# g stored unscaled, scaled by ScalarE after its load: one change to a planned attention and two-layer MoE kernel

## The chip, the cores and the metric

The kernel runs on one core of a Trainium2 chip. The metric is the device time of one execution, in microseconds; the figure for the kernel before is the median of three runs. A profile of one further execution gives the trace that is read here. The engines are named as in the profile: PE is TensorE's matmul, PEld its weight load, DVE is VectorE, ACT is ScalarE, POOL is GpSimd and SP is the queue that issues DMAs.

## The reference

Only the last part matters for this change. Attention (full attention over sequences shortened by four, plus a local one) gives x of 2304 tokens by 512; a first feed-forward layer with an ELU follows; then:

```python
def _moe2_ref(x, w_in, w_out, s, b) -> np.ndarray:
    h = x @ w_in
    r = np.maximum(h, 0.0)
    g = s * (r * r) + b
    return (g @ w_out).astype(np.float32)
```

Here w_in is 512 by 2048 and w_out 2048 by 512; s and b are one number each. All is float32. The kernel makes each product of float32 matrices from three products of a rounded high part and a remainder (high by high, low by high, high by low).

## The kernel before, in words

**A planner orders everything.** The program first collects operations (`op`, `act`, `on`, `load`), each with an engine or several to choose from, a length in microseconds that is written in by hand, the buffers that it reads and writes, and a due time. `Plan.emit` then moves due times back along the dependences, simulates the engines, and at each step gives an engine the operation with the earliest due time that is ready; if a more urgent one is not ready yet, an operation that is ready runs in the pause. The order so found is the order in each engine's instruction stream. Where the simulation sees TensorE idle, `keep_warm` (L1581) puts in matmuls of a tile of zeros, as many as fill the pause.

**The second feed-forward layer has two halves.** In the w2_in half (540 to 735 us) five groups of tokens pass through `unit`: groups 0, 1, 2 and 4 are pairs of 256-token blocks, group 3 is one block alone. A pair's four units each make seven products (`product`, L1453, twelve matmuls each, a scheme of Strassen's kind), in the order `ROW`. The first is copied out of PSUM by ScalarE (L1479), the others are summed by VectorE (`total`, L1463). The single block's unit (L1425) has plain products and returns before `product` is defined. Each finished h of 128 by 512 then goes through Relu on ScalarE (L1473 or L1435) and `finish`: a square (L1401, ScalarE or GpSimd; for one block in four Relu and square in one pass on VectorE, L1404), then a scale and shift by s and b (L1407), then a store to a buffer `gd` in DRAM (L1440, L1474). There are 72 such h. The next group's inputs are split into high and low parts by ScalarE (L1352) and VectorE (L1353).

The w2_out half (735 us to the end) is made of nine quads (`quad`), two for each pair, one for the single block. A quad loads four pieces of g of 128 by 1024 from `gd` (L1500, tile `gb`), and forms seven halves in the order `COL`: some are a loaded piece, others sums and differences of pieces (VectorE, L1527 to L1535). Each half is rounded to its high part by ScalarE (L1509), VectorE subtracts for the low part (L1510), and 24 matmuls follow (L1518). There are three buffers for these parts (`F`), and their places come free as the inputs `X` of the w2_in half are used up; the `gb` places and those of the sums lie where weights and h lay before. The weights of the w2_out half were prepared earlier and kept in DRAM; `kept_halves` loads them again (L1315) and splits them by ScalarE (L1282) and VectorE (L1283), as the places of the w2_in weights come free; pairs of weights 0 to 3 serve the first quad, 4 to 7 the second.

The due time of a quad is `time2[1, gi, qd]`, written `d` in the code; its loads are due 12 us earlier, its halves 2.84 us apart.

Of the kernel before, what the change touches and what calls it, by code (L numbers as in the profile page):

```python
# [299 lines left out]
def attn_moe_moe2(ctx, tc, q, k, v, w_in, w_out, w2_in, w2_out, s2, b2, mask, mask_d, out):  # L300
# [93 lines left out]
    def op(eng, us, fn, r=(), w=(), u=(), due=0.0, dma=0.0, nb=0.0, ffn=False, lock=False):  # L394
        plan.op(eng, us, fn, r, w, u, due, dma, nb, ffn, lock)
# [834 lines left out]
        have = {"dve": (0.08 + n / 960 + fixed, lambda: f(nc.vector)), "pool": (0.3 + n / 490 + fixed, lambda: f(nc.gpsimd))}  # L1230
        op(*[list(z) for z in zip(*[(e, *have[e]) for e in choice])], lock=True, **kw)

    def act(f, n, **kw):
        op("act", 0.1 + n / 1200, f, **kw)

    def parts():
        return Buf(None, "hi", None), Buf(None, "lo", None)
# [93 lines left out]
    def factors(kind, w, i):  # L1331
        return list(w[0 if i in MADE or i == (4 if kind else 3) else 1].part)
# [59 lines left out]
        return x  # L1392

    gd = {}

    def finish(h, made, stores, due, relu=False):

        q, g = Buf(None, "q", None), Buf(None, "g", None)
        if relu:
            op(["act", "pool"], [0.1 + 512 / 1200, 0.3 + 512 / 490],  # L1400
               [lambda: nc.scalar.activation(out=h(), in_=h(), func=ACTF.Square), lambda: nc.gpsimd.tensor_tensor(out=h(), in0=h(), in1=h(), op=ALU.mult)],  # L1401
               r=[made], w=[q], u=[h], due=due)
        else:
            on(lambda e: e.scalar_tensor_tensor(out=h(), in0=h(), scalar=0.0, in1=h(), op0=ALU.max, op1=ALU.mult), 512, ("dve",),  # L1404
               r=[made], w=[q], u=[h], due=due)
        op(["act", "dve"], [0.1 + 512 / 1200, 0.07 + 512 / 1920],
           [lambda: nc.scalar.activation(out=h(), in_=h(), func=ACTF.Identity, scale=sb2[:, 0:1], bias=sb2[:, 1:2]),  # L1407
            lambda: nc.vector.tensor_scalar(out=h(), in0=h(), scalar1=sb2[:, 0:1], scalar2=sb2[:, 1:2], op0=ALU.mult, op1=ALU.add)],
           r=[q, c_sb2], w=[g], u=[h], due=due, lock=True)
        for dst, fn, n in stores:  # L1410
            load(dst, n, fn, due, r=[g], u=[h], slow=SL)

    def unit(gi, u, x, w):

        d = time2[0, gi, u]
        if len(groups[gi]) == 1:
            for f in range(2):
# [12 lines left out]

                made = Buf(None, "made", None)
                op("pe", 24 * MM, pe, r=[*w[2 * u][1].part, *w[2 * u + 1][1].part, *x[0].part, *x[1].part], w=[e],
                   u=[w[2 * u][1], w[2 * u + 1][1], *x], due=d + f * 2 * PP, ffn=True)
                h = Buf(ar, "st", [128, 512])
                act(lambda h=h, e=e: nc.scalar.activation(out=h(), in_=e(), func=ACTF.Relu), 512, r=[e], w=[made], u=[h], due=d + f * 2 * PP)  # L1435
                stores = []
                for n in range(2):
                    dst = gd.setdefault((gi, 0, 2 * n + f), None) or dram_buf(f"gd{gi}_{2 * n + f}", [128, PAIRS, 128])
                    gd[gi, 0, 2 * n + f] = dst
                    stores.append((dst, lambda dst=dst, h=h, n=n: nc.sync.dma_start(  # L1440
                        out=dst.t[:, 2 * u:2 * u + 2, :], in_=h().rearrange("p (q n t) -> p q n t", q=2, n=2)[:, :, n]), 131072))
                finish(h, made, stores, d + f * 2 * PP + 10, True)
            return
        bank = {i: Buf(*{2: (ps_t, "at"), 5: (ps_h, "h"), 3: (ps_h, "h")}.get(i, (ps_a, "acc")), [128, 512]) for i in ROW}

        def product(i):

            def pe():
                ps = bank[i]()
                for q in range(2):  # L1450
                    for c in range(2):
                        for k, (wi, xi) in enumerate(PASSES):
                            nc.tensor.matmul(ps[:, q * 256:(q + 1) * 256], lhsT=factor(0, w[2 * u + q], i, wi, c),  # L1453
                                             rhs=x[i]()[:, xi].rearrange("p (c t) -> p c t", c=2)[:, c],
                                             start=q == c == k == 0, stop=q == c == 1 and k == 2)

            ws = [w[2 * u], w[2 * u + 1]]
            op("pe", 12 * MM, pe, r=[*factors(0, ws[0], i), *factors(0, ws[1], i), *x[i].part], w=[bank[i]],
               u=[x[i], *ws[0], *ws[1]], due=d + ROW.index(i) * PP, ffn=True)

        def total(i, a):
            h = Buf(ar, "st", [128, 512])
            op("dve", 0.08 + 512 / 940, lambda: nc.vector.tensor_tensor(out=h(), in0=bank[i](), in1=a(), op=ALU.add),  # L1463
               r=[bank[i], a], w=[h], due=d + ROW.index(i) * PP)
            return h

        def out(h, blk):
            dst = gd.get((gi, u // 2, blk)) or dram_buf(f"gd{gi}_{u // 2}_{blk}", [128, 2, 512])
            gd[gi, u // 2, blk] = dst
            made = h  # L1470
            if blk != 3:
                made = Buf(None, "made", None)
                act(lambda: nc.scalar.activation(out=h(), in_=h(), func=ACTF.Relu), 512, r=[h], w=[made], u=[h], due=d + 10)  # L1473
            finish(h, made, [(dst, lambda: nc.sync.dma_start(out=dst.t[:, u % 2], in_=h()), 262144)], d + 10, blk != 3)  # L1474

        for i in ROW:
            product(i)
        p1 = Buf(ar, "st", [128, 512])
        act(lambda: nc.scalar.activation(out=p1(), in_=bank[1](), func=ACTF.Copy), 512, r=[bank[1]], w=[p1], due=d)  # L1479
        out(total(2, p1), 0)  # L1480
        u2 = total(6, p1)
        u3, u4 = total(7, u2), total(5, u2)
        out(total(5, u3), 3)
        out(total(4, u3), 1)
        out(total(3, u4), 2)

    def quad(gi, qd, w, m):

        g = groups[gi]
        d = time2[1, gi, qd]  # L1490
        n_qd = len(g)
        tok = 128 * n_qd
        pairs = range(4 * qd, 4 * qd + 4) if n_qd == 2 else range(PAIRS)
# [3 lines left out]
        for blk in (1, 0, 2, 3):  # L1497
            a[blk], got[blk] = Buf(ar, "gb", [128, 1024]), Buf(None, "got", None)
            src = gd[gi, qd, blk]
            load(got[blk], 524288, lambda b=a[blk], src=src: nc.sync.dma_start(out=b(), in_=src.t.rearrange("p a t -> p (a t)")),  # L1500
                 d - 12, r=[src], u=[a[blk]], slow=SL)
        sq = Buf(ar, "sq", [128, 1024])
        s1, s2, s3, s4 = (Buf(None, f"s{i}", None) for i in range(1, 5))

        def half(i, src, r):
            k = COL.index(i)
            f = Buf(ar, "F", [128, 2, 1024], F32R)
            hi, lo = parts()
            act(lambda: nc.scalar.activation(out=f()[:, 0], in_=src(), func=ACTF.Copy), 1024, r=r, w=[hi], u=[f, src], due=d + 2 * k * PP)  # L1509
            on(lambda e: e.tensor_tensor(out=f()[:, 1], in0=src(), in1=f()[:, 0].bitcast(F32), op=ALU.subtract), 1024, ("dve", "pool"),  # L1510
               r=[*r, hi], w=[lo], u=[f, src], due=d + 2 * k * PP)

            def pe():
                for p, pair in enumerate(pairs):
# [9 lines left out]

        half(2, a[1], [got[1]])
        half(1, a[0], [got[0]])
        on(lambda e: e.tensor_tensor(out=sq(), in0=a[2](), in1=a[3](), op=ALU.add), 1024, r=[got[2], got[3]], w=[s1], u=[sq, a[2], a[3]], due=d + 4 * PP)  # L1527
        done = half(5, sq, [s1])
        on(lambda e: e.tensor_tensor(out=sq(), in0=sq(), in1=a[0](), op=ALU.subtract), 1024, r=[s1, got[0], *done], w=[s2], u=[sq, a[0]], due=d + 6 * PP)
        done = half(6, sq, [s2])  # L1530
        on(lambda e: e.tensor_tensor(out=a[2](), in0=a[0](), in1=a[2](), op=ALU.subtract), 1024, r=[s1, got[0], got[2]], w=[s3], u=[a[0], a[2]], due=d + 8 * PP)
        half(7, a[2], [s3])
        on(lambda e: e.tensor_tensor(out=sq(), in0=a[1](), in1=sq(), op=ALU.subtract), 1024, r=[s2, got[1], *done], w=[s4], u=[sq, a[1]], due=d + 10 * PP)
        half(3, sq, [s4])
        half(4, a[3], [got[3]])  # L1535
        if qd < n_qd - 1:
# [28 lines left out]
    for gi in range(len(groups)):  # L1565
        xs = inputs(gi, time2[0, gi, 0])
        for u in range(PAIRS // 2):
            unit(gi, u, xs, w2)
    w2 = [kept_halves(p, time2[1, 0, p // 4] - 12) for p in range(PAIRS)]
    for gi in order2:  # L1570
        ms = {}
        for qd in range(len(groups[gi])):
# [75 lines left out]
```

## Time and profile before

| | us |
|---|---|
| median of three runs (lowest, highest) | 926.96 (924.21, 929.6) |
| profiled execution, its own time | 927.33 |
| span of the profiled execution, first to last instruction | 925.6 |
| PE busy, 8460 matmuls | 910.1 |
| DVE busy | 700.8 |
| ACT busy | 556.7 |
| POOL busy | 392.0 |

The span is 1.73 us shorter than that execution's own time; what lies around it is not in the trace. Busy time of PE holds the matmuls of zeros too, and a matmul at a lower granted clock counts longer. Times in rows are microseconds from the start of the span.

### The profile page before, as it was taken

How to read it: one execution, taken by the hardware profiler on the slowest of the kernel's cores; microseconds unless marked ns; L12 is line 12 of the kernel's file. 1: busy time of each engine (PE TensorE's matmuls, PEld its weight loads, DVE VectorE, ACT ScalarE, POOL GpSimd, SP SyncE). 2: the span in 40 equal slices, each digit the busy share in tenths (PEclk: the TensorE clock that was granted, in tenths of full speed). 3: DMA queues.
4: the chain of work that ended last, by engine and by line, in shares of the span. 5: the costliest groups of instructions: out<-in, count | busy, mean ns of one | idle time of the engine just before them, and what ended most of it. 6: DMA issues, size and time to landing. Idle time of an engine off the chain costs nothing. (4 is left out here: it accounts for less than half of the span.)

```text
span 925.6 us, 21389 instructions
## 1 busy us (share of the span) xinstructions
PE 910.1 (98%) x8460; PEld 872.6 (94%) x8460; DVE 700.8 (76%) x1089; ACT 556.7 (60%) x1208; POOL 392.0 (42%) x353
## 2 busy tenths in 40 slices
PE   8999999999999999999999999998999989999998
PEld 5879999999999999999999999998999989999998
DVE  5467778888887888988635589989546889787775
ACT  5588776554554545444666669887687963433332
POOL 4567657798896769776536653000000000000000
PEclk9699999999999999999999999999999999999999
DMA  9739776544542425434302357898843783353411
GB/s 196 204 115 234 198 188 168 144 135 109 124 123 64 123 75 135 108 86 128 92 1 91 115 172 261 297 311 307 298 143 117 264 291 126 126 161 120 152 36 35
DMA packets 123524, 142.88 MB, mean 154 GB/s; under 512 B 50976, under 2 KB 93984, under 8 KB 123424
## 3 DMA queue, kind: packets, MB, share of 16 engines
q1 hardware_dynamic: 121632, 141.07, 51.7%
q8 instruction: 66, 1.08, 0.5%
q10 hardware_dynamic: 1792, 0.44, 0.2%
q14 instruction: 34, 0.28, 0.1%
HBM read 101.12 MB, written 40.37 MB: 153 GB/s over the span
## 5 line engine op out<-in xcount | busy, mean ns | idle before, releaser
L1034 PE MATMUL acc<-split,w 128*128 128x256 f32 x1728 | 234.9, 284 | 0.0
L1034 PEld LDWEIGHTS acc<-split,w 128*128 128x128 f32 x1728 | 216.5, 188 | 2.9 <-issue 1.9
L988 PE MATMUL h<-split,w 128*128 128x256 f32 x1488 | 205.2, 286 | 1.2 <-DVE work L1012 1.0
L988 PEld LDWEIGHTS h<-split,w 128*128 128x128 f32 x1488 | 188.7, 190 | 4.0 <-DVE work L1012 1.6
L413 POOL TENSOR_TENSOR split<-work,split 128x256 fp32r<-128x256 f32 (+2 forms) x154 | 137.0, 897 | 88.8 <-ACT split L405 72.8
L1518 PE MATMUL acc<-w,attn 128*128 128x256 f32 x864 | 107.1, 281 | 0.4 <-DVE attn L1510 0.4
L1518 PEld LDWEIGHTS acc<-w,attn 128*128 128x128 f32 x864 | 104.4, 189 | 0.8 <-DVE attn L1510 0.7
L405 ACT ACTIVATE split<-work 128x256 fp32r<-128x256 f32 (+2 forms) x162 | 66.7, 423 | 60.7 <-PE acc L1034 31.6
L1012 DVE SCALAR_TENSOR_TENSOR work<-work,h 128x256 f32<-128x256 f32 x124 | 50.6, 414 | 66.3 <-ACT work L1010 66.0
L1453 PE MATMUL acc<-attn,w 128*128 128x256 f32 x768 | 99.8, 283 | 0.6 <-ACT attn L1352 0.4
L1453 PEld LDWEIGHTS acc<-attn,w 128*128 128x128 f32 x768 | 95.2, 188 | 1.2 <-ACT attn L1352 0.6
L1008 ACT ACTIVATE work<-h 128x256 f32<-128x256 f32 x124 | 47.1, 380 | 75.8 <-PE h L988 48.7
L1509 ACT ACTIVATE attn<-split 128x1024 fp32r<-128x1024 f32 x43 | 45.5, 1060 | 74.5 <-PE acc L1518 29.8
L413 POOL TENSOR_TENSOR work<-work 128x896 f32<-128x896 f32 (+1 forms) x41 | 68.0, 1666 | 6.2 <-DVE work L930 5.5
L1510 DVE TENSOR_TENSOR attn<-split,attn 128x1024 fp32r<-128x1024 f32 x43 | 52.4, 1221 | 19.9 <-ACT attn L1509 19.6
L930 DVE TENSOR_REDUCE work<-work 128x128 f32<-128x896 f32 x36 | 63.5, 1789 | 4.8 <-POOL work L413 4.8
L1010 ACT ACTIVATE work<-work 128x256 f32<-128x256 f32 x144 | 60.0, 416 | 3.9
L1518 PE MATMUL h<-w,attn 128*128 128x256 f32 x432 | 56.1, 286 | 3.1 <-ACT attn L1509 2.4
L1518 PEld LDWEIGHTS h<-w,attn 128*128 128x128 f32 x432 | 54.1, 194 | 3.5 <-ACT attn L1509 2.6
L1407 ACT ACTIVATE split<-split,sb 128x512 f32<-128x512 f32 x64 | 50.7, 809 | 5.6 <-DVE split L1404 4.8
L1453 PE MATMUL h<-attn,w 128*128 128x256 f32 x384 | 51.5, 282 | 0.0
L1283 POOL TENSOR_TENSOR w<-work,w 128x1024 fp32r<-128x1024 f32 x16 | 40.5, 2540 | 20.9 <-ACT w L1282 20.9
(191 smaller groups left out, 1559.6 us busy)
## 6 DMA issues: line engine op xcount, KB each, us to landing
gd<-split SPq DMA_DIRECT2D x57, 256.0 KB
work<-gd SPq DMA_DIRECT2D x20, 512.0 KB
work<-in_moe_w_in_dram SPq DMA_DIRECT2D x16, 512.0 KB
work<-in_moe_w_out_dram SPq DMA_DIRECT2D x16, 512.0 KB
work<-in_moe_w_in_dram SPq DMA_DIRECT2D x8, 1024.0 KB
work<-in_moe_w_out_dram SPq DMA_DIRECT2D x8, 1024.0 KB
split<-gd SPq DMA_DIRECT2D x16, 512.0 KB
work<-in_k_dram SPq DMA_DIRECT2D x17, 320.0 KB
```

Source lines behind the costliest of these rows:

```text
L405: a = (0.11 + n / 1200, lambda: nc.scalar.activation(out=out(), in_=src(), func=ACTF.Copy, scale=scale))
L413: f = lambda e: lambda: e.tensor_tensor(out=out(), in0=in0(), in1=in1(), op=alu)
L930: op("dve", 0.07 + 14 * D / 546, lambda: nc.vector.tensor_reduce(out=vo()[:, WD + j * D:WD + (j + 2) * D].rearrange("p (j d) -> p j d", j= ...
L988: nc.tensor.matmul(ps(), lhsT=w()[:, wpart, 0, c * 128:(c + 1) * 128], rhs=x.at(xpart)[:, c, :], start=first and i == 0, stop=last and i = ...
L1008: op("act", ta + 0.07, lambda: nc.scalar.activation(out=e(), in_=ps(), func=ACTF.Relu, scale=-1.0), r=[ps], w=[r1], u=[e], due=due)
L1010: op("act", ta, lambda: nc.scalar.activation(out=e(), in_=e(), func=ACTF.Exp, scale=-1.0), r=[r1], w=[r2], u=[e], due=due)
L1012: op("dve", td, lambda: nc.vector.scalar_tensor_tensor(out=e(), in0=e(), scalar=-1.0, in1=ps(), op0=ALU.add, op1=ALU.max), r=[r2, ps], w=[ ...
L1034: nc.tensor.matmul(acc()[:, c * N:(c + 1) * N], lhsT=wo[:, cc * 128:(cc + 1) * 128], rhs=g(), start=first and c == 0, stop=end and c == 1)
L1407: [lambda: nc.scalar.activation(out=h(), in_=h(), func=ACTF.Identity, scale=sb2[:, 0:1], bias=sb2[:, 1:2]), lambda: nc.vector.tensor_scala ...
L1453: nc.tensor.matmul(ps[:, q * 256:(q + 1) * 256], lhsT=factor(0, w[2 * u + q], i, wi, c), rhs=x[i]()[:, xi].rearrange("p (c t) -> p c t", c ...
L1510: on(lambda e: e.tensor_tensor(out=f()[:, 1], in0=src(), in1=f()[:, 0].bitcast(F32), op=ALU.subtract), 1024, ("dve", "pool"), r=[*r, hi], ...
L1518: nc.tensor.matmul(m[i]()[:, c * 256:(c + 1) * 256], lhsT=f()[:, xi, o:o + 128], rhs=factor(1, w[pair], i, wi, 0), start=qd == 0 and p == ...
```

## The change

The scale and shift leave `finish`: g is stored as the bare square. In each quad, every loaded piece is scaled and shifted in place by ScalarE (128 by 1024, 36 passes) before anything reads it. In the plan, Relu and Square get 0.1 us more length; the new pass gets 1.30 us. The halves of the first quad are due 6 us earlier (`e`), the kept weights of pairs 4 to 7 are due 8 us later, and the loads of group 0's pieces also depend on a buffer `mark`, which a product of group 3 is to write. The lambdas' argument is renamed where `e` is now a number.

```diff
-    def act(f, n, **kw):
-        op("act", 0.1 + n / 1200, f, **kw)
+    def act(f, n, fixed=0.0, **kw):
+        op("act", 0.1 + n / 1200 + fixed, f, **kw)
...
+    mark = Buf(None, "mark", None)
     def finish(h, made, stores, due, relu=False):
-        q, g = Buf(None, "q", None), Buf(None, "g", None)
+        g = Buf(None, "g", None)
         if relu:
-            op(["act", "pool"], [0.1 + 512 / 1200, 0.3 + 512 / 490],
+            op(["act", "pool"], [0.2 + 512 / 1200, 0.3 + 512 / 490],
...
-               r=[made], w=[q], u=[h], due=due)
+               r=[made], w=[g], u=[h], due=due)
...
-        op(["act", "dve"], [0.1 + 512 / 1200, 0.07 + 512 / 1920],
-           [lambda: nc.scalar.activation(out=h(), in_=h(), func=ACTF.Identity, scale=sb2[:, 0:1], bias=sb2[:, 1:2]),
-            lambda: nc.vector.tensor_scalar(out=h(), in0=h(), scalar1=sb2[:, 0:1], scalar2=sb2[:, 1:2], op0=ALU.mult, op1=ALU.add)],
-           r=[q, c_sb2], w=[g], u=[h], due=due, lock=True)
...
-                act(lambda h=h, e=e: nc.scalar.activation(out=h(), in_=e(), func=ACTF.Relu), 512, r=[e], w=[made], u=[h], due=d + f * 2 * PP)
+                act(lambda h=h, e=e: nc.scalar.activation(out=h(), in_=e(), func=ACTF.Relu), 512, fixed=0.1, r=[e], w=[made], u=[h], due=d + f * 2 * PP)
...
-            op("pe", 12 * MM, pe, r=[*factors(0, ws[0], i), *factors(0, ws[1], i), *x[i].part], w=[bank[i]],
+            op("pe", 12 * MM, pe, r=[*factors(0, ws[0], i), *factors(0, ws[1], i), *x[i].part], w=[bank[i], mark] if (gi, u, i) == (3, 0, 1) else [bank[i]],
...
         d = time2[1, gi, qd]
+        e = d - 6 * ((gi, qd) == (order2[0], 0))
...
-                 d - 12, r=[src], u=[a[blk]], slow=SL)
+                 d - 12, r=[src, mark] if gi == order2[0] else [src], u=[a[blk]], slow=SL)
+            scaled = Buf(None, "scaled", None)
+            act(lambda b=a[blk]: nc.scalar.activation(out=b(), in_=b(), func=ACTF.Identity, scale=sb2[:, 0:1], bias=sb2[:, 1:2]), 1024,
+                fixed=0.35, r=[got[blk], c_sb2], w=[scaled], u=[a[blk]], due=d - 4)
+            got[blk] = scaled
...
-            act(lambda: nc.scalar.activation(out=f()[:, 0], in_=src(), func=ACTF.Copy), 1024, r=r, w=[hi], u=[f, src], due=d + 2 * k * PP)
+            act(lambda: nc.scalar.activation(out=f()[:, 0], in_=src(), func=ACTF.Copy), 1024, r=r, w=[hi], u=[f, src], due=e + 2 * k * PP)
...
-    w2 = [kept_halves(p, time2[1, 0, p // 4] - 12) for p in range(PAIRS)]
+    w2 = [kept_halves(p, time2[1, 0, p // 4] - (12, 4)[p // 4]) for p in range(PAIRS)]
```

The subtractions and sums of a quad (L1510, L1527 to L1535) get `e` in place of `d` in the same way.

## Rows read from the trace of the kernel before

**Rows 1.** Timeline of PE alone: start, length, line, tile, count [idle before, releaser].
```profile
586.34 3.04 PE L1453 MATMUL at<-attn,w 128*128 128x256 f32 x24
...
596.69 1.60 PE L1453 MATMUL h<-attn,w 128*128 128x256 f32 x12
...
629.81 1.60 PE L1453 MATMUL at<-attn,w 128*128 128x256 f32 x12
...
634.58 1.70 PE L1453 MATMUL at<-attn,w 128*128 128x256 f32 x12 [2.55 <-DVE split L1463]
...
662.13 3.04 PE L1453 MATMUL acc<-attn,w 128*128 128x256 f32 x24
...
670.74 0.72 PE L1581 MATMUL at<-wz 128*128 128x512 bf16 x4
671.97 23.30 PE L1425 MATMUL acc<-attn,w 128*128 128x256 f32 x192 [0.51 <-ACT split L1479]
...
735.42 2.98 PE L1518 MATMUL at<-w,attn 128*128 128x256 f32 x24
...
744.34 0.50 PE L1518 MATMUL h<-w,attn 128*128 128x256 f32 x2 [2.38 <-ACT attn L1509]
745.60 4.41 PE L1518 MATMUL h<-w,attn 128*128 128x256 f32 x22 [0.76 <-DVE attn L1510]
...
751.40 5.94 PE L1518 MATMUL acc<-w,attn 128*128 128x256 f32 x48
```

**Rows 2.** The chain that ended last, in order of time: start, length, work.
```profile
760.19 2.85 PE acc L1518 x24
```

**Rows 3.** Timeline of ACT before B's copy and D's third half.
```profile
631.81 1.51 ACT L1407 ACTIVATE split<-split,sb 128x512 f32<-128x512 f32 x2
633.22 0.57 ACT L1479 ACTIVATE split<-acc 128x512 f32<-128x512 f32 x1
...
743.25 1.04 ACT L1509 ACTIVATE attn<-split 128x1024 fp32r<-128x1024 f32 x1
```

**Rows 4.** Timeline of DVE in the w2_out half.
```profile
744.32 1.23 DVE L1510 TENSOR_TENSOR attn<-split,attn 128x1024 fp32r<-128x1024 f32 x1 [2.42 <-ACT attn L1509]
...
810.77 1.22 DVE L1510 TENSOR_TENSOR attn<-split,attn 128x1024 fp32r<-128x1024 f32 x1
```

**Rows 5.** Stretches: length, busy PE, PEld, DVE, ACT, POOL, clock, DMA share, GB/s.
```profile
586.00:596.00 10.00, 9.40 (x76) 8.73 (x75) 9.17 (x17) 8.20 (x13) 0.00 (x0) 1.00 0.80 271
...
636.20:664.90 28.70, 28.70 (x241) 28.65 (x239) 20.45 (x35) 18.86 (x29) 0.00 (x0) 1.00 0.92 331
...
739.20:745.60 6.40, 3.26 (x24) 2.85 (x25) 3.94 (x5) 6.30 (x10) 0.00 (x0) 1.00 0.75 248
745.60:751.60 6.00, 6.00 (x31) 5.13 (x32) 6.00 (x6) 4.48 (x5) 0.00 (x0) 0.72 1.08 365
...
783.00:922.50 139.50, 139.50 (x1176) 139.32 (x1175) 103.59 (x101) 51.63 (x51) 0.00 (x0) 1.00 0.32 104
...
735.40:763.00 27.60, 24.01 (x180) 22.53 (x178) 23.67 (x24) 20.50 (x24) 0.00 (x0) 0.94 0.82 292
```

**Rows 6.** Stretches of L1407 alone: length, ACT busy, clock, DMA share, GB/s.
```profile
628.00:634.00 6.00, 2.31 (x3) 1.00 0.74 290
...
728.00:744.00 16.00, 5.58 (x7) 1.00 0.74 252
```

**Rows 7.** Groups by line: count, busy, mean ns of one, idle before by releaser.
```profile
L1407 ACT ACTIVATE split<-split,sb 128x512 f32<-128x512 f32 x64 | 50.7, 809 | 5.6 <-DVE split L1404 4.8
L1509 ACT ACTIVATE attn<-split 128x1024 fp32r<-128x1024 f32 x43 | 45.5, 1060 | 74.5 <-PE acc L1518 29.8 <-DVE split L1529 20.6 <-PE h L1518 14.4
L1352 ACT ACTIVATE attn<-split 128x512 fp32r<-128x512 f32 x23 | 13.5, 618 | 3.2 <-PE acc L1453 2.4 <-PE at L1453 0.8
```

**Rows 8.** Timeline of the queue SP: first loads of the first and second quad.
```profile
637.49 1.07 SPq L1500 DMA_DIRECT2D work<-gd  x2
...
738.15 0.32 SPq L1500 DMA_DIRECT2D split<-gd  x1
```

More of the change, by code (lines that the diff above doesn't have):

```diff
@@ L1394, in attn_moe_moe2 @@
     gd = {}
+    mark = Buf(None, "mark", None)
     def finish(h, made, stores, due, relu=False):
-        q, g = Buf(None, "q", None), Buf(None, "g", None)
+        g = Buf(None, "g", None)
         if relu:
-            op(["act", "pool"], [0.1 + 512 / 1200, 0.3 + 512 / 490],
+            op(["act", "pool"], [0.2 + 512 / 1200, 0.3 + 512 / 490],
                [lambda: nc.scalar.activation(out=h(), in_=h(), func=ACTF.Square), lambda: nc.gpsimd.tensor_tensor(out=h(), in0=h(), in1=h(), op=ALU.mult)],
-               r=[made], w=[q], u=[h], due=due)
+               r=[made], w=[g], u=[h], due=due)
         else:
             on(lambda e: e.scalar_tensor_tensor(out=h(), in0=h(), scalar=0.0, in1=h(), op0=ALU.max, op1=ALU.mult), 512, ("dve",),
-               r=[made], w=[q], u=[h], due=due)
-        op(["act", "dve"], [0.1 + 512 / 1200, 0.07 + 512 / 1920],
-           [lambda: nc.scalar.activation(out=h(), in_=h(), func=ACTF.Identity, scale=sb2[:, 0:1], bias=sb2[:, 1:2]),
-            lambda: nc.vector.tensor_scalar(out=h(), in0=h(), scalar1=sb2[:, 0:1], scalar2=sb2[:, 1:2], op0=ALU.mult, op1=ALU.add)],
-           r=[q, c_sb2], w=[g], u=[h], due=due, lock=True)
+               r=[made], w=[g], u=[h], due=due)
         for dst, fn, n in stores:
@@ L1472, in out @@
                 made = Buf(None, "made", None)
-                act(lambda: nc.scalar.activation(out=h(), in_=h(), func=ACTF.Relu), 512, r=[h], w=[made], u=[h], due=d + 10)
+                act(lambda: nc.scalar.activation(out=h(), in_=h(), func=ACTF.Relu), 512, fixed=0.1, r=[h], w=[made], u=[h], due=d + 10)
             finish(h, made, [(dst, lambda: nc.sync.dma_start(out=dst.t[:, u % 2], in_=h()), 262144)], d + 10, blk != 3)
@@ L1508, in half @@
             hi, lo = parts()
-            act(lambda: nc.scalar.activation(out=f()[:, 0], in_=src(), func=ACTF.Copy), 1024, r=r, w=[hi], u=[f, src], due=d + 2 * k * PP)
-            on(lambda e: e.tensor_tensor(out=f()[:, 1], in0=src(), in1=f()[:, 0].bitcast(F32), op=ALU.subtract), 1024, ("dve", "pool"),
-               r=[*r, hi], w=[lo], u=[f, src], due=d + 2 * k * PP)
+            act(lambda: nc.scalar.activation(out=f()[:, 0], in_=src(), func=ACTF.Copy), 1024, r=r, w=[hi], u=[f, src], due=e + 2 * k * PP)
+            on(lambda eng: eng.tensor_tensor(out=f()[:, 1], in0=src(), in1=f()[:, 0].bitcast(F32), op=ALU.subtract), 1024, ("dve", "pool"),
+               r=[*r, hi], w=[lo], u=[f, src], due=e + 2 * k * PP)
             def pe():
@@ L1526, in quad @@
         half(1, a[0], [got[0]])
-        on(lambda e: e.tensor_tensor(out=sq(), in0=a[2](), in1=a[3](), op=ALU.add), 1024, r=[got[2], got[3]], w=[s1], u=[sq, a[2], a[3]], due=d + 4 * PP)
+        on(lambda eng: eng.tensor_tensor(out=sq(), in0=a[2](), in1=a[3](), op=ALU.add), 1024, r=[got[2], got[3]], w=[s1], u=[sq, a[2], a[3]], due=e + 4 * PP)
         done = half(5, sq, [s1])
-        on(lambda e: e.tensor_tensor(out=sq(), in0=sq(), in1=a[0](), op=ALU.subtract), 1024, r=[s1, got[0], *done], w=[s2], u=[sq, a[0]], due=d + 6 * PP)
+        on(lambda eng: eng.tensor_tensor(out=sq(), in0=sq(), in1=a[0](), op=ALU.subtract), 1024, r=[s1, got[0], *done], w=[s2], u=[sq, a[0]], due=e + 6 * PP)
         done = half(6, sq, [s2])
-        on(lambda e: e.tensor_tensor(out=a[2](), in0=a[0](), in1=a[2](), op=ALU.subtract), 1024, r=[s1, got[0], got[2]], w=[s3], u=[a[0], a[2]], due=d + 8 * PP)
+        on(lambda eng: eng.tensor_tensor(out=a[2](), in0=a[0](), in1=a[2](), op=ALU.subtract), 1024, r=[s1, got[0], got[2]], w=[s3], u=[a[0], a[2]], due=e + 8 * PP)
         half(7, a[2], [s3])
-        on(lambda e: e.tensor_tensor(out=sq(), in0=a[1](), in1=sq(), op=ALU.subtract), 1024, r=[s2, got[1], *done], w=[s4], u=[sq, a[1]], due=d + 10 * PP)
+        on(lambda eng: eng.tensor_tensor(out=sq(), in0=a[1](), in1=sq(), op=ALU.subtract), 1024, r=[s2, got[1], *done], w=[s4], u=[sq, a[1]], due=e + 10 * PP)
         half(3, sq, [s4])
```

## The prediction

> **What bounds the kernel now.** I read the page of the profile first: its busy shares give TensorE 910.1 of 925.6 us, so any gain must come out of TensorE's own holes. Two things hide holes from that figure. The plan fills a pause that it foresees with matmuls on a tile of zeros (L1581), which count as busy, and a matmul at a lower granted clock is busy for longer. So I went to the timeline of TensorE alone and measured real matmuls against an undisturbed rate. In the w2_in half 24 matmuls take 1.44 us more than 12 (3.04 against 1.60), 0.120 us each [rows 1]; in the w2_out half the chain of waits counts 2.85 us for 24, 0.1187 us each [rows 2]. Against these rates four holes stand out [rows 1]:
>
> A, 586.34 to 596.69: 10.35 us for 72 matmuls that need 8.64, so 1.71 lost.
> B, 629.81 to 634.58: 4.77 for 12 that need 1.44, 3.33 lost.
> C, 662.13 to 671.97: 9.84 for 60 that need 7.20, 2.64 lost.
> D, 735.42 to 751.40, the change from the w2_in to the w2_out half: 15.98 for 72 that need 8.55, 7.43 lost.
>
> Together 15.1 us. After D the chain of waits is matmuls alone, with no hole [rows 2], and before 540 us the plan's input is the same in both kernels except for due times that move by about 0.1 us at its border. So 15.1 us is the most the change can give.
>
> What ends each hole? The waits at B, C and D lead to ScalarE. In B TensorE resumes when VectorE's sum L1463 is through, after 2.55 us of waiting [rows 1]; that sum needs bank 1's copy L1479, which ScalarE begins only at 633.22 [rows 3]. In C the first matmul of the single block waits for the copy L1479 itself [rows 1]. In D it waits 2.38 us for the rounding L1509 of the third half [rows 1, 3], and VectorE is idle 2.42 us for the same pass [rows 4]. ScalarE was not waiting for anything there: it was busy 6.30 of the 6.40 us from 739.20 to 745.60 [rows 5]. In the six microseconds around B it ran three passes of L1407 (and three each around A and C, in the same view), and seven between 728 and 744 [rows 6]. L1407 is the pass that the change takes out of the w2_in half.
>
> **The change, part by part.**
>
> *Removed: 72 scale-and-shift passes, 512 wide.* Sixty-four, and eight more on another buffer, 0.809 us each by the groups of instructions [rows 7], so 58 us of ScalarE. Two of them back to back delay the next instruction by 1.41 us (631.81 to 633.22) [rows 3]: 0.705 us each. What this is worth, hole by hole:
> A: three passes, 2.1 us, lie ahead of the splits L1352. But VectorE is busy 9.17 of 10 us there [rows 5], so it may give nothing, and at most 1.71. I take 0.9, about the middle.
> B: three passes, 2.1 us, stand ahead of the copy. Between 0 and 3.33; I take 2.1, the passes' own length.
> C: three passes, 2.1 us, precede the copy. The wait at the end (0.51 us) and the planned filler ahead of it (0.72 us) go [rows 1], 1.2; the other 1.4 comes after splits L1352, for which ScalarE itself waits on TensorE [rows 7], and stays. Between 0 and 2.64; I take 1.2.
> D: seven passes, 4.9 us. L1509 would then start at 738.3 instead of 743.25 [rows 3], and with its own 1.04 and VectorE's 1.23 the third half is ready at about 740.6, before TensorE has gone through the first two (735.42 + 48 x 0.1187 = 741.1). The wait of 2.38 us and the 0.76 behind it go. So does a second loss: after that wait 22 matmuls took 4.41 us where 2.61 were due [rows 1], with the granted clock at 0.72 of full over that stretch [rows 5], a mean of its two levels, 1.2 and 2.4 GHz. That is 3.14 + 1.80 = 4.94 us. The Trainium skill ("TensorE: Matmul & The Clock Gate", Part 1) says that the slow clock is the default and activity lifts it; the trace agrees, since the clock is 1.00 before the wait and low behind it.
> The other 2.49 us of D I leave in. VectorE is busy 23.67 us from 735.40 to 763.00 [rows 5], when the second quad starts. Without D that stretch is 20.2 us. So 3.5 us of its work has to run sooner or later than now. Three of the splits L1283 for the second quad's later halves (1024 wide like the L1510 of 1.23 us [rows 4]) can run later, which makes it just fit. Bounds for D: 0 and 7.43; I take 4.94.
>
> *Added: 36 scale-and-shift passes, 1024 wide, in place after the loads of g.* No such pass is in the trace. The 512-wide one takes 0.809; a plain pass grows from 0.618 at 512 to 1.060 at 1024 [rows 7]; so I take 1.25 us, 45 us in all, between 1.06 (a plain pass) and 1.62 (two of 512). By the Trainium skill ("ScalarE: Activation LUTs", What ACT_TABLE_LOAD costs), with its figures for immediates, for each pointer operand and per element, an estimate for this pass is 1.23 us. It would leave the sum as it is.
> Where do they lie? ScalarE is 37% busy in the w2_out half (51.63 of 139.50 us) [rows 5]; four passes per quad of 19.9 us add 25%. A half's rounding is 1.06 and VectorE's part 1.22 against 2.85 us of matmuls, and in the middle of the half the two are done about 2.1 us ahead of TensorE (the L1510 of 810.77 to 811.99 [rows 4] makes the operand of matmuls that start at about 814.1). One added pass in front of a rounding costs it 1.25 at most. It stays hidden: 0. For the first quad, the loads are issued from 637.49 on [rows 8], and ScalarE is idle for 9.8 of the 28.7 us from 636.20 to 664.90 [rows 5]; the plan lets a ready instruction run in a pause whatever its due time, so these four passes (5.0 us) lie there. For the second quad the loads start at 738.15 [rows 8], when the last buffers of the w2_in half come free, 17 us ahead of its new start at about 755.5. Price 0; if that cover fails, see the rivals.
>
> *Moved.* The stores of g wait for one pass less, so they are issued about 0.8 us sooner and free their buffers sooner; the queue SP has nothing late behind them. The first quad's roundings are due 6 us earlier and the second quad's kept weights 8 us later. This puts the halves that TensorE wants first ahead of splits wanted later, on ScalarE and VectorE alike; it is part of what I count in D. The loads of those weights are due later too, behind the loads of g on SP; their buffers stay, so the price is 0 unless VectorE falls behind. The changed lengths in the plan (Relu, Square) put its picture nearer to the trace, where a pass 512 wide takes 0.62 us [rows 7] against 0.53 planned. I give this no value of its own, bounds -1.4 and +1.4, the size of one planned filler.
>
> *The mark.* It is written by a product of group 3. Group 3 is the single block, whose unit returns before any product is made. So nothing writes the mark and the loads wait for nothing new. If it did bind, the loads would go out near 672 instead of 637, still 60 us ahead: the same time.
>
> **Sum.** 0.9 + 2.1 + 1.2 + 4.9 = 9.1 us. The profiled execution: span 925.6, own time 927.33, 1.73 more. 925.6 - 9.1 + 1.73 = 918.2. That execution lies 0.37 above the median of the runs, 926.96; so I predict 918.0, rounded. Likeliest case alone: 912 (all of 15.1) to 922.
>
> **The rivals.**
> *VectorE is the real bound.* For it: 9.17 of 10 us busy at A, 23.67 of 27.60 around D [rows 5]. Then A and B keep their length, C gives 1.2 and D only half of VectorE's idle 3.9 us: 3.2 us, 923.8. Against it: VectorE's longest wait in D is for ScalarE [rows 4].
> *The work only changes place.* The first quad's four passes, 4 x 1.25 = 5.0 us, run at their due time, just ahead of the roundings, where 4.9 us was taken out. D stays; A, B and C give 4.2: 922.8. It decides if no pause before 724 takes them. Against it: the loads at 637 [rows 8].
> *Slower: the passes queue up ahead of a rounding in the w2_out half.* A quad's four passes are due before the last half of the quad ahead. If all four stand in front of one rounding, that is 5.0 us against the 2.1 us of lead: 2.9 us of wait in each of the seven quads from the third on, 20 us: 938. It decides when more than one pass stands in front of a rounding (2 x 1.25 > 2.1). Against it: 74.5 us of idle time ahead of 43 roundings, 1.7 us each [rows 7], which take the passes one at a time, since loads are issued as soon as a buffer is free, a quad ahead.
>
> **How the numbers follow.** Chances: forecast 0.66, VectorE 0.13, change of place 0.11, slower 0.10. Half a per cent (4.6 us, about what a measurement of this kernel can tell from no change) puts the border of faster at 922.3. The forecast lies below it; of the VectorE case I put 0.06 below and 0.07 above; the change of place lies within. Faster 0.72, same 0.18, slower 0.10. The range 912 to 925 holds everything but the slow case and a little at the edges.
>
> **What would show it.** Right: no L1407 left, and ScalarE's new line in the quads at about 1.25 us, with the first four before 700; TensorE's hole at the change of halves under 3 us with a granted clock near 1.0; B and C shorter; matmuls in the w2_out half still at 2.85 us for 24. Wrong: a hole of the old size at the change of halves, with VectorE busy through it (first rival) or ScalarE's new passes in it (second), or waits of matmuls for L1509 or L1510 after 760 (third); or new fillers of zeros, if the new plan places pauses that the old one did not have.

## The result, and the profile after

The changed kernel takes 912.77 us (median of 6 runs, 908.04 to 916.02) against 928.55 us for the kernel before (median of 6 runs): ratio 0.983, 95% interval 0.980 to 0.987. The prediction was 918.0, range 912 to 925; its sign and its place were right, its size was too small (9.1 us forecast, 15.8 measured).

Single runs of either kernel scatter by 5 to 8 us, and in the profiled runs nearly all of that comes from the first 60 us (last section). So the kernels are compared below by a stretch that leaves it out: from the first product of the w2_in half to the end of the span. Before, it is 925.6 - 540.06 = 385.54 us, of which 195.36 in the w2_in half (to 735.42). After, it is 914.2 - 544.43 = 369.77 us, of which 187.20 in the w2_in half (to 731.63). The difference, 15.77 us, is the whole difference of the medians.

The page of the kernel after, busy time of each engine, then its w2_in and its w2_out half by stretches (length; busy PE, PEld, DVE, ACT, POOL; clock, DMA share, GB/s):

```profile
PE 903.8 (99%) x8433; PEld 870.1 (95%) x8433; DVE 700.4 (77%) x1089; ACT 546.5 (60%) x1173; POOL 389.8 (43%) x352
```
```profile
544.43:731.63 187.20, 187.20 (x1563) 187.20 (x1561) 156.12 (x234) 118.82 (x181) 14.15 (x6) 1.00 0.76 260
731.63:914.20 182.57, 179.58 (x1514) 179.38 (x1512) 143.25 (x141) 109.48 (x107) 0.00 (x0) 1.00 0.40 135
```

TensorE is busy for all of the 187.20 us, with no matmul of zeros in them: 1536 products at 0.120 us are 184.3, and 24 of the layer before, run in between, are the other 2.9. The timeline of TensorE after, at the places that answer to [rows 1]:

```profile
590.51 3.04 PE L1450 MATMUL at<-attn,w 128*128 128x256 f32 x24
...
599.15 1.60 PE L1450 MATMUL h<-attn,w 128*128 128x256 f32 x12
...
632.27 1.60 PE L1450 MATMUL at<-attn,w 128*128 128x256 f32 x12
633.71 3.04 PE L1450 MATMUL acc<-attn,w 128*128 128x256 f32 x24
...
661.07 3.04 PE L1450 MATMUL acc<-attn,w 128*128 128x256 f32 x24
...
668.27 23.20 PE L1422 MATMUL acc<-attn,w 128*128 128x256 f32 x192
...
731.63 3.01 PE L1520 MATMUL at<-w,attn 128*128 128x256 f32 x24
734.48 3.01 PE L1520 MATMUL acc<-w,attn 128*128 128x256 f32 x24
737.32 3.01 PE L1520 MATMUL h<-w,attn 128*128 128x256 f32 x24
740.17 5.86 PE L1520 MATMUL acc<-w,attn 128*128 128x256 f32 x48
```

A is now 8.64 us for its 72 matmuls, B 1.44 for 12, C 7.20 for 60 and D 8.54 for 72: each is what the undisturbed rate asks, to 0.01 us. All four holes are gone, not parts of them.

The new passes, by the timeline of ScalarE (the first quad's four, then the first of the second quad) and by the groups of instructions:

```profile
655.22 1.23 ACT L1501 ACTIVATE work<-work,sb 128x1024 f32<-128x1024 f32 x1
...
665.06 1.23 ACT L1501 ACTIVATE work<-work,sb 128x1024 f32<-128x1024 f32 x1
...
667.38 2.36 ACT L1501 ACTIVATE work<-work,sb 128x1024 f32<-128x1024 f32 x2
...
731.81 1.04 ACT L1511 ACTIVATE attn<-split 128x1024 fp32r<-128x1024 f32 x1
...
738.37 2.37 ACT L1501 ACTIVATE split<-split,sb 128x1024 f32<-128x1024 f32 x2
```
```profile
L1501 ACT ACTIVATE work<-work,sb 128x1024 f32<-128x1024 f32 x20 | 24.5, 1233 | 2.3 <-DMA work<-gd 2.3
L1511 ACT ACTIVATE attn<-split 128x1024 fp32r<-128x1024 f32 x43 | 45.5, 1059 | 35.6 <-DVE split L1531 13.2 <-PE acc L1520 9.3 <-PE h L1520 4.7
```

One pass is 1.23 us (1.25 taken). The first quad's four lie between 655 and 670, one or two at a time in pauses, as forecast, and the third half's rounding starts at 731.81, 0.18 us after TensorE enters the w2_out half; before, it came 7.8 us after [rows 1, 3]. The idle time ahead of these 43 roundings has fallen from 74.5 [rows 7] to 35.6 us: that is where most of the added passes went.

VectorE had been the doubt. Its stretches of 30.4 us up to the change of halves, first of the kernel before, then of the one after, and the 19.9 us behind it, after:

```profile
705.00:735.40 30.40, 30.40 (x255) 30.40 (x255) 23.02 (x31) 28.70 (x42) 0.00 (x0) 1.00 0.66 211
```
```profile
701.20:731.60 30.40, 30.40 (x255) 30.40 (x255) 26.24 (x34) 25.51 (x35) 0.00 (x0) 1.00 0.72 240
731.60:751.50 19.90, 19.90 (x170) 19.90 (x169) 19.75 (x20) 17.49 (x20) 0.00 (x0) 1.00 0.90 331
```

VectorE has 3.2 us more done by the time TensorE enters the w2_out half (26.24 against 23.02), because ScalarE hands its operands over earlier: in these two stretches its waits for ScalarE add up to 3.4 us before and to 0.5 us after. Then it is busy 19.75 of 19.90 us, and it just keeps up.

### The profile page after: what moved, and what is told of

It reads as the page before. It is cut to its first block, busy times and chain, and to the rows that moved or that the text cites. A ratio compares the mean times of both kernels' runs of the same rounds, so it can differ in the third digit from the quotient of the medians.

```text
span 914.2 us, 21282 instructions
## 1 busy us (share of the span) xinstructions
PE 903.8 (99%) x8433; PEld 870.1 (95%) x8433; DVE 700.4 (77%) x1089; ACT 546.5 (60%) x1173; POOL 389.8 (43%) x352
## 4 chain that ended last, share of the span: by engine, by line
PE 86%; DVE 5%; DMA 3%; POOL 2%; issue 2%; ACT 1%; SPq 1%; DVEq 0%; POOLq 0%; ACTq 0%
PE acc L1034 19%; PE h L988 17%; PE acc L1520 11%; PE acc L1450 10%; PE h L1520 6%; PE h L1450 5%; PE at L1520 3%; PE at L1450 3%; PE acc L1422 3%; PE acc L988 2%; DVE work L930 1%; DMA w<-in_v_dram 1%; PE at L822 1%; PE acc L1583 1%; PE h L822 1%
## 5 line engine op out<-in xcount | busy, mean ns | idle before, releaser
L413 POOL TENSOR_TENSOR split<-work,split 128x256 fp32r<-128x256 f32 (+2 forms) x154 | 137.7, 901 | 90.7 <-ACT split L405 76.7
L413 POOL TENSOR_TENSOR work<-work 128x896 f32<-128x896 f32 (+1 forms) x41 | 67.2, 1647 | 5.8 <-DVE work L930 5.4
L1511 ACT ACTIVATE attn<-split 128x1024 fp32r<-128x1024 f32 x43 | 45.5, 1059 | 35.6 <-DVE split L1531 13.2
L1520 PE MATMUL h<-w,attn 128*128 128x256 f32 x432 | 54.2, 281 | 0.0
L1470 ACT ACTIVATE split<-split 128x512 f32<-128x512 f32 x44 | 27.5, 628 | 35.2 <-DVE split L1460 34.8
```

The lines of the kernel that those rows point to most:

```text
L413: f = lambda e: lambda: e.tensor_tensor(out=out(), in0=in0(), in1=in1(), op=alu)
L1520: nc.tensor.matmul(m[i]()[:, c * 256:(c + 1) * 256], lhsT=f()[:, xi, o:o + 128], rhs=factor(1, w[pair], i, wi, 0), start=qd == 0 and p == ...
```

## The experiments

Theory 1: ScalarE's queue was the cause; the 72 passes stood in front of what TensorE needed next, and where they went (pauses of ScalarE) they cost nothing. Theory 2, the rival: the plan was at fault; with measured lengths or better due times the passes would have done no harm where they were. Two more questions are inside: how near VectorE is to its limit, and whether the added passes can be felt. In the table "w2_in" is the time from the first product of that half to the first of the w2_out half, "rest" from there to the end of the span, both from one profile; the medians are of the timed runs, the ratio is to the kernel before on the same chip with its 95% interval. Spans are given to 0.1 us, so "rest" and "sum" are no finer. Four streams (move only, no lengths, last group without the pass, pass twice) ran most or all of the w2_out half at a shorter pitch (24 matmuls in 2.82 us instead of 2.85, last section), which makes their "rest" 1.5 to 2 us shorter for a reason that has nothing to do with holes; where holes are compared, their own lengths are used.

| kernel | w2_in | rest | sum | median, us | ratio |
|---|---|---|---|---|---|
| before | 195.36 | 190.18 | 385.54 | 928.55 | |
| after | 187.20 | 182.57 | 369.77 | 912.77 | 0.983 (0.980 to 0.987) |
| move only | 187.20 | 184.04 | 371.24 | 913.44 | 0.983 (0.980 to 0.985) |
| lengths only | 192.54 | 189.24 | 381.78 | 925.62 | 0.996 (0.994 to 0.998) |
| due times only | 195.46 | 189.20 | 384.66 | 927.78 | 0.999 (0.997 to 1.002) |
| after, no due times | 187.20 | 184.69 | 371.89 | 912.52 | 0.982 (0.977 to 0.988) |
| after, no lengths | 187.19 | 182.32 | 369.51 | 911.00 | 0.983 (0.979 to 0.986) |
| before, last group without the pass | 195.48 | 183.97 | 379.45 | 921.62 | 0.994 (0.991 to 0.997) |
| after, no pass at all | 187.20 | 182.57 | 369.77 | 911.83 | 0.984 (0.980 to 0.987) |
| after, pass on VectorE | 187.19 | 190.86 | 378.05 | 918.34 | 0.991 (0.987 to 0.995) |
| after, pass twice | 187.47 | 184.56 | 372.03 | 915.18 | 0.987 (0.983 to 0.992) |
| after, mark binds | 187.20 | 182.57 | 369.77 | 912.21 (one run) | |
| after again | 187.19 | 182.63 | 369.82 | 912.14 | 0.984 (0.981 to 0.987) |
| after, with zeros | 187.40 | 182.93 | 370.33 | 908.31 (one run) | |

**The move alone.**

```diff
 (to the kernel before)
-        op(["act", "dve"], ..., r=[q, c_sb2], w=[g], u=[h], due=due, lock=True)
...
+            act(lambda b=a[blk]: nc.scalar.activation(out=b(), in_=b(), func=ACTF.Identity, scale=..., bias=...), 1024,
+                r=[got[blk], c_sb2], w=[scaled], u=[a[blk]], due=d - 4)
```

> The kernel before with the scale and shift moved behind the loads of g, and nothing else: no new lengths for Relu and Square (the new pass gets 0.1 + 1024/1200), no own due times. Measured by the stretch from the first product of the w2_in half to the end of the span: 385.5 us before, 369.8 after (187.2 + 182.6, no hole). Theory 1, the removed passes were what kept ScalarE late: at most 374 us, total about 913 to 917. Theory 2, the planner's wrong lengths and due times made the holes and the passes only sat in them: 380 us or more, total 922 or more.

371.24 us and 913.44: theory 1. The w2_in half is whole at once. At the change of halves the plan leaves two pauses with zeros; timeline of TensorE:

```profile
730.21 3.01 PE L1520 MATMUL acc<-w,attn 128*128 128x256 f32 x24
733.05 0.66 PE L1583 MATMUL at<-wz 128*128 128x512 bf16 x3
733.52 3.10 PE L1520 MATMUL h<-w,attn 128*128 128x256 f32 x24
736.46 2.88 PE L1583 MATMUL at<-wz 128*128 128x512 bf16 x14
739.15 5.88 PE L1520 MATMUL acc<-w,attn 128*128 128x256 f32 x48
```

From the first zeros to the next real matmul they cost 0.47 and 2.69 us, 3.2 together. (The sum shows only 1.5 of it, since behind them this stream ran its matmuls at the shorter pitch.)

**The lengths alone.**

```diff
 (to the kernel before: plan lengths only)
-op(["act", "pool"], [0.1 + 512 / 1200, ...
+op(["act", "pool"], [0.2 + 512 / 1200, ...
-op(["act", "dve"], [0.1 + 512 / 1200, 0.07 + 512 / 1920],
+op(["act", "dve"], [0.38 + 512 / 1200, 0.35 + 512 / 1920],
 (and fixed=0.1 for both Relus)
```

> The kernel before with measured lengths in the plan and nothing else: Relu and Square 0.53 to 0.53 + 0.1, the scale and shift 0.53 to 0.81 on ScalarE (0.34 to 0.62 on its alternative, VectorE). The passes stay where they were. Theory 1: ScalarE's work is the same, so the holes stay and only turn from waits into planned matmuls of zeros; stretch 382 to 389 us, total within 4 us of before. Theory 2: the order gets right once the lengths are; stretch 374 or less, total 917 or less.

381.78 us, just under the bottom of what theory 1 gave and far from theory 2's 374. As expected, no wait is left and planned zeros stand instead. They are not all in the old places: C has none, and a new pause of 1.55 us stands right before the w2_out half (732.51). Near B's place (36 to 48 matmuls ahead of it), by the timeline of TensorE:

```profile
626.55 2.17 PE L1581 MATMUL at<-wz 128*128 128x512 bf16 x10
628.53 1.68 PE L1453 MATMUL acc<-attn,w 128*128 128x256 f32 x12
630.05 0.39 PE L1581 MATMUL at<-wz 128*128 128x512 bf16 x1
```

Right lengths are worth 3.8 us while ScalarE is late, less than a quarter of the change. With the work moved they are worth about 1 us of pauses: with the old due times 3.2 us of pauses without the lengths and 2.1 with them, with the new due times 1.2 and none. The sums (371.24 and 371.89; 369.51 and 369.77) hide this, because both streams without the lengths ran at the shorter pitch.

**The due times alone.**

```diff
 (to the kernel before)
+        e = d - 6 * ((gi, qd) == (order2[0], 0))
...
-    w2 = [kept_halves(p, time2[1, 0, p // 4] - 12) for p in range(PAIRS)]
+    w2 = [kept_halves(p, time2[1, 0, p // 4] - (12, 4)[p // 4]) for p in range(PAIRS)]
```

> The kernel before with the own due times only (first quad's roundings 6 us earlier, kept weights of pairs 4 to 7 due 8 us later). Theory 1: the three holes of the w2_in half stay (about 8 us), the hole at the change of halves shrinks in part, since seven passes of L1407 are still there, 7.4 to 4 us or so; stretch 381 to 386. Theory 2: the hole at the change of halves goes, stretch 378 or less.

384.66: A, B and C stay (8.3 us over 187.20), and the hole at the change of halves falls only from 7.6 to 6.6 us, less than the 3 us or so that I had thought. From 739.00 to 747.50 ScalarE is busy 8.47 of 8.50 us, so a due time finds no free moment there. From 751.50 to 768.00 it is VectorE that is full (16.50 of 16.50 us, ScalarE 9.61), and 3.6 us of planned zeros stand there: with the roundings first and the passes left in place, the end of this hole is VectorE's.

**The changed kernel without its due times.**

```diff
 (to the kernel after)
-        e = d - 6 * ((gi, qd) == (order2[0], 0))
+        e = d
-... - (12, 4)[p // 4]) for p in range(PAIRS)]
+... - 12) for p in range(PAIRS)]
```

> The changed kernel without the own due times (first quad's roundings and the kept weights as before). If the move alone relieves ScalarE enough, the change of halves has a hole of 2 us at most: stretch 369.8 to 372, total about 913 to 915. If the due times are what lets VectorE, busy 19.75 of 19.90 us there after the change, serve the first quad first, the hole is 4 us or more and the granted clock falls behind it: stretch 374 to 378, total 917 to 921.

371.89 us: 2.1 us come back, planned zeros at 733.01 and 736.30, at the upper edge of the first alternative. Once ScalarE has room, the due times are worth 2 us.

**The changed kernel without the lengths.**

```diff
 (to the kernel after)
-in_=h(), func=ACTF.Relu), 512, fixed=0.1, ...      -[0.2 + 512 / 1200, ...      -fixed=0.35, r=[got[blk], ...
+in_=h(), func=ACTF.Relu), 512, ...                 +[0.1 + 512 / 1200, ...      +r=[got[blk], ...
```

> The changed kernel without the measured lengths: Relu and Square planned at 0.53, the new pass at 0.95 instead of 1.30; own due times kept. Theory 1, ScalarE has slack enough now that the plan's error does not matter: stretch 369.8 to 371.5, total as the changed kernel. Rival: the short lengths let the plan set work too close at the change of halves, with 2 us or more of waits there: 372 to 376.

369.51 us, a little below what theory 1 gave. One planned pause of 1.2 us appears (760.56 to 761.79); behind it the shorter pitch makes up for it. Its median, 911.0 (910.04 to 912.7), cannot be told from the changed kernel's; no version clearly beats it.

**One group's passes left out of the kernel before.**

```diff
 (to the kernel before)
-        op(["act", "dve"], ..., r=[q, c_sb2], w=[g], u=[h], due=due, lock=True)
+        if last:          # gi == 4
+            g = q
+        else:
+            op(["act", "dve"], ..., r=[q, c_sb2], w=[g], u=[h], due=due, lock=True)
```

> The kernel before with the scale and shift left out for the last pair of the w2_in half (group 4) only, so a fifth or so of the pieces of g stays unscaled in the output; groups 0 to 3 keep the pass. If each hole hangs on the passes that lie right before it: the holes A to C stay (about 8 us) and the one at the change of halves falls from 7.4 to 3 us or less; stretch from the first w2_in product to the end about 377 to 381 us. If the change of halves is bound by VectorE, it keeps 5 us or more: 383 or more.

This ties each hole to the passes of its own group. B is untouched:

```profile
631.13 1.60 PE L1456 MATMUL at<-attn,w 128*128 128x256 f32 x12
632.58 0.77 PE L1584 MATMUL acc<-wz 128*128 128x512 bf16 x5
635.89 1.70 PE L1456 MATMUL at<-attn,w 128*128 128x256 f32 x12 [2.54 <-DVE split L1466]
```

The w2_in half keeps its length (195.48 us); the rest falls from 190.18 to 183.97, of which nearly 2 us are the shorter pitch. The hole at the change of halves falls from 7.4 to 3.2 us, two pauses of zeros as in the move alone, a little more than the 3 us expected; at the longer pitch the sum would lie near 381, the top of the range (an estimate from the two pitches). In the kernel with the work moved, the same 3.2 us go with the plan's numbers: 2.1 with the lengths, none with the due times as well.

**No pass at all.**

```diff
 (to the kernel after)
-            act(lambda b=a[blk]: ... Identity ..., due=d - 4)
-            got[blk] = scaled
```

> The changed kernel with the scale and shift left out altogether, so g is the bare square. If the 36 added passes are hidden, the stretch is 369.8 us as in the changed kernel and the total differs by less than 4 us. If they cost something that better order made up for, it is shorter; the rate of the matmuls leaves no room for that below 369.5.

Both halves are as long as the changed kernel's, as finely as the span is given (0.1 us). The 36 passes are hidden entirely.

**The passes on VectorE.**

```diff
 (to the kernel after)
-            act(lambda b=a[blk]: ... Identity ..., fixed=0.35, ..., due=d - 4)
+            op("dve", 0.08 + 1024 / 1920, lambda b=a[blk]: nc.vector.tensor_scalar(out=b(), in0=b(), scalar1=..., scalar2=...,
+               op0=ALU.mult, op1=ALU.add), r=[got[blk], c_sb2], w=[scaled], u=[a[blk]], due=d - 4, lock=True)
```

> The changed kernel with the 36 passes on VectorE (planned at 0.61 us each) instead of ScalarE. VectorE is busy 19.75 of the 19.90 us after the change of halves. If it is at its limit there, the eight passes of the first two quads, 5 us or more, come back as a hole: stretch 374 to 380. If it had room, 370 to 372.

378.05 us. The timeline of TensorE, and the stretches ahead of the hole and in it:

```profile
747.38 8.21 PE L1583 MATMUL at<-wz 128*128 128x512 bf16 x38
755.40 3.10 PE L1520 MATMUL acc<-w,attn 128*128 128x256 f32 x24
```
```profile
727.40:747.40 20.00, 20.00 (x171) 19.95 (x170) 19.93 (x20) 11.63 (x14) 4.44 (x2) 1.00 0.92 337
747.40:755.60 8.20, 8.20 (x41) 3.84 (x40) 7.18 (x4) 2.95 (x3) 4.34 (x2) 1.00 0.16 62
```

The w2_in half is as good as ever, but the change of halves loses 8 us. VectorE is busy 19.93 of the 20 us before the hole (the pass of 2.89 us below among them) while ScalarE has time to spare. So VectorE does bind there, the moment it gets more work: the changed kernel stands right at that edge.

The 8 us are not the passes' own length. Not eight passes lie here, as I had expected, but the second quad's four (733.01, 737.14, 737.87, 744.27), 0.81 us each but for the last; the first quad's four ran at 653 to 665. The plan also gave subtractions of this quad to GpSimd, and beside them VectorE's instructions took longer: a pass 2.89 us, and a sum at L1529, which takes 1.22 elsewhere in this run, 3.26. The timeline of GpSimd and VectorE:

```profile
742.96 6.41 POOL L1512 TENSOR_TENSOR attn<-split,attn 128x1024 fp32r<-128x1024 f32 x2 [174.36 <-ACT attn L1511]
744.27 2.89 DVE L1501 TENSOR_SCALAR work<-work,sb 128x1024 f32<-128x1024 f32 x1
747.20 3.26 DVE L1529 TENSOR_TENSOR split<-work 128x1024 f32<-128x1024 f32 x1
```

TensorE does not wait behind the 38 zeros, so the pause has the length that the plan foresaw. How its 8.2 us divide between the four passes and the changed order is not shown.

**The passes twice.**

```diff
 (to the kernel after)
+            act(lambda b=a[blk]: nc.scalar.activation(out=b(), in_=b(), func=ACTF.Copy), 1024,
+                fixed=0.15, r=[scaled], w=[again], u=[a[blk]], due=d - 4)
+            got[blk] = again
```

> The changed kernel with a plain copy in place on ScalarE behind each scale and shift, 36 more passes of about 1.06 us (ScalarE then about 16.6 of 19.9 us in a quad). It tests the rival that was to end slower. If passes in front of a rounding eat a lead of 2.1 us, matmuls wait in most quads: stretch 380 us or more. If ScalarE takes them one at a time in its pauses, the quads stay whole and only the change of halves suffers, where ScalarE was 17.49 of 19.90 us busy: 371 to 376.

372.03 us: one pause at the change of halves (742.56, 2.85 us to the next real matmul) and one of about a microsecond in a later quad. In the middle of the half ScalarE has 71.34 us of work in 93.00; TensorE waits for nothing there, and the later pause (832.79), which the plan foresaw, is all that it loses:

```profile
787.00:880.00 93.00, 93.00 (x792) 92.48 (x791) 73.65 (x70) 71.34 (x70) 3.50 (x1) 1.00 0.35 117
```

The rival that was to end slower, a queue of passes in front of a rounding, does not form even with twice the passes.

**The mark made to bind.**

```diff
 (to the kernel after)
-w=[bank[i], mark] if (gi, u, i) == (3, 0, 1) else [bank[i]],
+w=[bank[i]],
-... *x[0].part, *x[1].part], w=[e],
+... *x[0].part, *x[1].part], w=[e, mark] if (u, f) == (0, 0) else [e],
```

> The changed kernel with the mark written by the single block's first product, so that the loads of group 0's pieces do wait for it. The prediction said that the time stays the same: stretch 369.8 us, the loads issued after about 668 us instead of around 640.

369.77 us, the same. The first load goes out at 666.49 instead of 644.80, and nothing is late. As written, the mark is without effect; with effect, it is without cost.

**The changed kernel again, and with a few zeros.**

```diff
 (to the kernel after, second run only)
+                if qd == 0 and k <= 1 and gi == order2[0]:
+                    for _ in range(4):
+                        nc.tensor.matmul(m[i]()[:, :128], lhsT=wz, rhs=wz, start=True, stop=True)
```

> The changed kernel once more, unaltered. Its stretch should again be 187.2 us in the w2_in half with no wait and no planned zeros. In the w2_out half 24 matmuls took 2.85 us in its first profile, but 2.82 in those of three of the variants. If that pitch belongs to the instruction stream, this profile shows 2.85 and 182.6 us again; if it belongs to the execution, it may show 2.82 and 180.6. Total as before, 908 to 916.

> The changed kernel with four matmuls of zeros, 128 wide, in front of each of the first two halves of the first quad: the plan does not know them. If a short pause of real matmuls is what moves the pitch from 2.85 to 2.82 us for 24 (it moved behind planned zeros in two variants, and did not in one), the halves behind them run at 2.82; if not, 2.85 and the stretch grows by the zeros' own 0.5 us.

Again 187.19 and 182.63, with the same pitch of 2.85 us for 24; the zeros do not move it, and cost 0.56 us over the first profile's stretch. For the pitch, see the last section.

## Why the prediction was right in sign and too small

**What bounds: right.** Holes of TensorE, hidden by zeros and by a low clock, were all there was to gain, and ScalarE's queue made them. The most that the change could give was put at 15.1 us; it gave 15.77. I had ended B and D where the next matmuls start; those behind a hole are a little slower as well (12 in 1.53 us behind B, where 1.44 is due), as are the 12 ahead of A (584.70 to 586.34), and that is part of the rest.

**A, B and C: mechanism right, size too small.** Forecast 0.9 + 2.1 + 1.2 = 4.2; measured 195.36 - 187.20 = 8.16, and the move alone gives all of it: the holes whole (1.71 + 3.33 + 2.64 = 7.68) and 0.5 of slower matmuls around them. The failed step is that each hole was priced by the passes that stood right before it: B at "the passes' own length", 2.1 of 3.33; C with 1.4 that "stays", and stayed at none; for A I let VectorE's 9.17 of 10 us cap the gain, and that share was not a bound.

What the price left out are passes further back. ScalarE had no queue when it came to B: it had waited 1.96 us for a sum of VectorE, until 628.71. It was VectorE that came late, held up by ScalarE before. In the 31.81 us up to the product in front of the hole (629.81 before, 632.27 after) VectorE waited 4.0 us for ScalarE in the kernel before (the longest wait, 2.1 us, for a copy behind passes of L1407 at 618.23, 620.13 and 620.84) and not at all after, and got less done. The timeline of ScalarE before; VectorE's waits in that stretch before (us in total, times, longest); the stretch before, then after:

```profile
628.71 0.64 ACT L1473 ACTIVATE split<-split 128x512 f32<-128x512 f32 x1 [1.96 <-DVE split L1463]
```
```profile
DVE split L1463 <- ACT split L1479: 2.9, 2, 2.1
DVE split L1463 <- ACT work L1479: 0.7, 1, 0.7
DVE attn L1353 <- ACT attn L1352: 0.4, 1, 0.4
```
```profile
598.00:629.81 31.81, 31.81 (x267) 31.81 (x266) 27.61 (x49) 26.52 (x41) 0.00 (x0) 1.00 0.98 329
```
```profile
600.46:632.27 31.81, 31.81 (x267) 31.81 (x266) 30.86 (x54) 20.39 (x34) 0.00 (x0) 1.00 0.98 340
```

So the copy L1479 came 3.4 us after the start of that product, and comes 1.8 us before it now (L1476 at 630.44): 5.2 us sooner, of which the three passes right before it are 2.1 at most. The 25.13 us ahead of C are alike: VectorE's waits for ScalarE fall from 6.1 to 1.0 us. Ahead of A they do not fall (1.5 and 1.9 us); there ScalarE itself was nearly full, 29.99 of 31.84 us, against 20.36 after.

**D: the step that failed is "The other 2.49 us of D I leave in".** Forecast 4.9; measured 190.18 - 182.57 = 7.61. I argued that VectorE could not do its 23.67 us of work in the shorter stretch, while deferring splits would just make it fit; the rest I left in by caution. It did fit, but by working ahead: VectorE did 3.2 us more before the change of halves than in the kernel before, and was full behind it. The parts are separable: with the move alone 3.2 us of zeros stayed, with the lengths too 2.1, and with the due times as well none; with the due times and without the lengths, 1.2 us in the second quad. The first rival was thus wrong for this change and right about the edge: put the passes on VectorE and 8 us come back, and with the due times alone VectorE fills the end of the hole.

**Added passes at 0: right**, shown by leaving them out. **The second rival** (the first quad's passes in the crowded stretch) fell with the passes at 655 to 670. **The third** did not form, even with the passes doubled. **The mark**: right on both counts.

**Lengths given no value, bounds -1.4 and +1.4: within the bounds.** In the changed kernel they are worth 1.1 to 1.2 us of planned pauses. Alone, in the kernel before, they would have given 3.8 us.

## What to carry to other kernels

When the engine that bounds shows 98% busy, subtract fillers and slow stretches first and price the holes against an undisturbed rate; that gives the most a change can bring, and here the change brought all of it. Work that must be done anyway is cheapest on an engine's pauses in a later stage: look for the stage in which the engine in front of the bound is late, and move its deferrable work behind a load. Price such work not only in the hole right behind it: at B part of its delay reached TensorE through VectorE, which had waited for ScalarE further back. Once that engine has room, ask which engine is full next and give its urgent work the earlier due times; that was worth 2 us here after the move, and 1 us without it.

## What was not expected of the hardware

**The first 60 us set the scatter of whole runs.** The first product of the w2_in half starts at 540.06 us before, 544.43 after, and 535.37 with the pass twice, though what comes ahead of it is planned from the same work up to its last few us. From 30 to 60 us, the same three kernels, one stretch each:

```profile
30.00:60.00 30.00, 29.66 (x337) 23.65 (x336) 15.01 (x34) 18.86 (x57) 15.67 (x17) 0.78 0.51 142
```
```profile
30.00:60.00 30.00, 29.86 (x287) 23.12 (x286) 14.03 (x28) 17.67 (x48) 15.10 (x17) 0.70 0.44 121
```
```profile
30.00:60.00 30.00, 29.18 (x377) 22.73 (x375) 18.64 (x42) 22.69 (x71) 20.06 (x20) 0.98 0.62 176
```

The lag is there at the end of this stretch and hardly grows behind it: the last of one group of 288 matmuls at L750 starts at 71.6 us before, 76.2 after and 67.5 with the pass twice, 8.7 us between the extremes, where the first product of the w2_in half shows 9.1. It goes with the granted clock of 0.78, 0.70 or 0.98 of full, but not with the clock alone: in the first 30 us TensorE also waited 2.5 us for GpSimd (L807, for L413) in the kernel after, and 0.3 with the pass twice. The profiled run of the changed kernel drew the worst of these; that is why its span is only 11.4 us shorter. What decides the clock there was not tried.

**Two pitches at full clock.** In the w2_out half 24 matmuls take 2.85 us in some instruction streams and 2.82 in others, 2 us over the half. It changed behind planned zeros in the move alone, without the lengths and with the last group's passes left out, was short from the start with the pass twice, and stayed long behind planned zeros without the due times and with the pass on VectorE, and behind the added zeros. Two profiles of the changed kernel both showed 2.85. What sets it stays open.

**Zeros held the clock.** With the passes on VectorE, TensorE ran 8.2 us of zeros and the granted clock stayed at 1.00, the upper of its two levels (2.4 GHz); in the kernel before, behind D's wait, it was 0.72 [rows 5]. So a planned pause cost its own length, and D's wait, which the plan did not foresee, cost 1.8 us more. Not every such wait did: behind B's, 2.55 us long, the clock stayed at 1.00.

```profile
634.58:640.00 5.42, 5.42 (x44) 5.37 (x45) 5.08 (x8) 4.32 (x7) 0.00 (x0) 1.00 0.63 212
```

**VectorE beside GpSimd.** With the passes on VectorE, its instructions took 2.89 and 3.26 us beside GpSimd's subtractions, and 0.81 and 1.22 us elsewhere (rows of that experiment); with the pass twice, a subtraction of VectorE took 2.84 us instead of 1.22 beside one of GpSimd, right ahead of the pause at 832.79.
